# Second batch's rows 8 to 15 of the first stage in the prologue, fewer warm-up products, and loads on other queues

## The chip, the cores and the metric

The kernel runs on one core of one Trainium2 chip. The metric is the device time of the whole program in microseconds (us). Five engines work side by side, each with its own in-order instruction stream: TensorE (PE in the profile, with PEld for its weight loads), VectorE (DVE), ScalarE (ACT), GpSimd (POOL) and SyncE (SP). ACT, POOL and SP also issue DMAs; an issue on one of them stands in that engine's stream, and what is behind it waits with it.

## The reference

The input `x` has 8 batches of 3008 rows of 256 float32. Along the 3008 rows it is Fourier transformed, multiplied by a complex filter and transformed back; then an expert layer with 2048 hidden units runs over all 24064 rows.

```python
X = np.fft.rfft(x, axis=1)                    # (8, 1505, 256)
Y = X * (filt_r + 1j * filt_i)[None]
y = np.fft.irfft(Y, n=3008, axis=1).astype(np.float32).reshape(24064, 256)
h = y @ w_in                                  # (24064, 2048); the weights come in 64-bit floats
g = h - np.tanh(h)
out = (g @ w_out).astype(np.float32)          # (24064, 256)
```

## The kernel before

The length 3008 is 64 times 47. The transform of a batch has four steps: a 64-point step over every residue `r` (**first**), an exchange through DRAM (`ct1[b]`), a 47-point step there and back with the filter between (**middle**), another exchange (`ct2[b]`), and a last 64-point step (**last**, products `pu`, PSUM to SBUF tile `ut`). Residues `r` and 47-r are treated together, so there are 24 rows of them (`NH`), worked in groups of four (`NX` = 6 groups for the first step). The expert layer then takes `ut` in 48 groups of up to 512 rows, each in four units: `up` makes the hidden units (tile `h`), `shrink` applies h - tanh h with ACT and DVE, `down` multiplies by the second weights. From the second group on `up` uses seven products in place of eight (sums of weight blocks, `sums`, made on DVE); the first group (units 0 to 3) uses `up_plain` and `down_plain`.

The 64-bit weights are converted to float32 by hand: `converted` loads a piece (`raw`, `raws`, or halves of the tiles `ft` and `a2`), ACT makes its exponent (L181, tile `top` or `xy`), and DVE does six steps (L183 to L201). There are 16 pieces: `jobs[0]` to `jobs[4]` in the prologue (`early`, stepped by `convert`), `jobs[5]` on between the instructions of units 0 to 5 (`late`).

The **prologue** (pool `pro`, PSUM pool `ps0` with eight banks) does batch 0 by a way of its own. A few products on a constant (`warmer`, L1081) run first. Three chunks of eight rows of `x` (`xs[0..2]`) and of the matrix `f_d` (`fh`, copied to `f0` by DVE, L1188) are loaded over SP, ACT and POOL; `first0(c)` multiplies chunk c on PE (L1071), ACT copies it. The load of the filter on POOL waits for the first half of the third chunk (`gate`, L1197). Then come seven groups of frequencies: transposes (`across`, L1094), the 47-point step (`forth`, L428), the filter (`filtered`, DVE and POOL, L447 to L456), and the way back (`back0`, L1139 and L1141, and for the last group `back`, L478). ACT copies each of its results to a tile `e1` (four buffers, L1144 and L481), and a DMA stores that in `ct2[0]`. `rest` (L1129) loads `ct2[0]` back as the tile `e2` of the first `last`: frequencies 0 to 24 early, the last seven when the last stores have landed. In between, `first1` (L1227) does rows 0 to 7 of batch 1 with `f0`, ACT copies them, and SP stores them in `ct1[1]`. Eight more products of `warmer` follow, then `last` of the first group, then four products named `pt` (L1374), then unit 0 (L719).

The other rows of batch 1, and all of batch 2, are done by `first` (L308) between the units: ten jobs, taken from a list of due places (`due`). Everything is recorded in program order (a manual schedule), and the engines keep that order; the framework adds the semaphores. A pool that takes over the PSUM of a closed pool first waits for the closed pool's last readers: here `pu` waits for the last ACT copy of the prologue.

Of the kernel before, what the change touches and what calls it, by code (L numbers as in the profile page):

```python
# [21 lines left out]
SG = 5  # L22
# [95 lines left out]
def kernel(  # L118
# [144 lines left out]
    def load_x(t, b, r, n):  # L263

        nc.sync.dma_start(t[0:64, 0:n, :], dram(x.tensor, (b * SEQ + r) * DM,
                                                [[NR * DM, 64], [1, n * DM]]))
        lo = 1 if r == 0 else 0
        if lo:
            nc.sync.dma_start(t[64:128, 0, :], dram(x.tensor, b * SEQ * DM,
                                                    [[NR * DM, 64], [1, DM]]))  # L270
        nc.sync.dma_start(t[64:128, lo:n, :], dram(x.tensor, (b * SEQ + NR - r - lo) * DM,
                                                   [[NR * DM, 64], [-DM, n - lo], [1, DM]]))
        return t
# [310 lines left out]
    def last(i, z, held=False):  # L584
# [13 lines left out]
        even, odd = banks  # L598
        for k in (1, 0) if held else (1,):
# [3 lines left out]
        u4 = ut.rearrange("p h (j n) -> p h j n", n=128)  # L603
        m = sum(w == 128 for w in widths(c))
# [3 lines left out]
        if i == 0:  # L608
            uts[i] = (ut, None, w)
            yield  # L610
            return
# [420 lines left out]
    with tc.tile_pool(name="tr", bufs=2) as tr, tc.manual_schedule():  # L1032
# [16 lines left out]
        with tc.tile_pool(name="pro", bufs=1) as pro, \  # L1049
# [122 lines left out]
            for c in range(3):  # L1172
# [4 lines left out]
                (ACT if c else nc.sync).dma_start(fh, f_d[:, 512 * c:512 * c + 512])  # L1177
# [44 lines left out]
            def first1(x1):  # L1222

                for r in range(0, 8, 2):
                    pf = z0("pf", [128, 2, DM])
                    for k in range(2):
                        nc.tensor.matmul(pf[:, k], f0[:, r + k], x1[:, r + k],  # L1227
                                         start=True, stop=True)
                    if r % 4 == 0:
                        two = (tr.tile([128, 2, 2, DM], F32, tag="a1", bufs=1, name="a1") if r else  # L1230
                               buffer("xy").rearrange("p (m n) c -> p m n c", m=2))
                    a1 = two[:, r // 2 % 2]
                    ACT.copy(a1, pf)
                    nc.sync.dma_start(
# [288 lines left out]
```

## Time and profile before

| | us |
|---|---|
| median of 3 runs (lowest to highest) | 2541.87 (2540.63 to 2543.5) |
| the profiled execution | 2542.18 |
| its span, first to last instruction | 2540.3 |

| engine | busy us | share of the span |
|---|---|---|
| PE | 2522.6 | 99% |
| PEld (weight loads, beside PE) | 2173.1 | 86% |
| DVE | 1935.6 | 76% |
| ACT | 1694.2 | 67% |
| POOL | 1532.0 | 60% |

A row of the timeline gives the start, the length, the engine, the line, what it writes and reads, how many instructions are merged, and in brackets the idle time before it with what ended it. A float32 product shows as two matmul instructions (a product of 128x256 as two of 128x256). The prologue ends and the first unit of the expert layer begins at about 80 us.

### The profile page before, as it was taken

Reading aid. Unit: us, or ns where it says so; the run is one execution under the profiler, and the core shown is the slowest. Engines: PE = TensorE matmul, PEld = TensorE weight load, DVE = VectorE, ACT = ScalarE, POOL = GpSimd, SP = SyncE. Lnnn points to the kernel's source line nnn. Section 1 sums busy time; section 2 is a strip of 40 time slices with the busy share of each in tenths; the row PEclk is TensorE's granted clock in tenths of the full one; section 3 lists DMA queues with packets and bytes.
Section 4 is the critical chain, followed back from the end, with each engine's and each line's share of the span. In section 5 each row is a group of like instructions: output and inputs, shape, how many; then the busy total and the mean of one; then the engine's idle time right before and its main releaser. Section 6 shows DMA issues by size and latency. Waiting matters only on the chain.

```text
span 2540.3 us, 44575 instructions
## 1 busy us (share of the span) xinstructions
PE 2522.6 (99%) x17072; PEld 2173.1 (86%) x17072; DVE 1935.6 (76%) x2270; ACT 1694.2 (67%) x2551; POOL 1532.0 (60%) x1112
## 2 busy tenths in 40 slices
PE   9999999999999999999999999999999999999998
PEld 8678889888898888988888888898889888898887
DVE  6888877988678876888669886698866888555555
ACT  4666666667666766676667666666666666666665
POOL 5255665667556765676656665666655666455552
PEclk9999999999999999999999999999999999999999
DMA  9854224422343323342334322343123322110110
GB/s 245 261 150 117 65 54 100 112 65 53 86 108 91 82 69 89 80 112 59 80 87 105 87 56 72 96 111 89 36 72 84 92 66 53 26 31 19 25 22 19
DMA packets 333664, 211.37 MB, mean 83 GB/s; under 512 B 231645, under 2 KB 305531, under 8 KB 329793
## 3 DMA queue, kind: packets, MB, share of 16 engines
q1 hardware_dynamic: 319091, 184.93, 29.8%
q0 software_dynamic: 11120, 16.16, 2.3%
q10 hardware_dynamic: 3230, 7.34, 0.9%
q8 instruction: 136, 2.23, 0.4%
q14 instruction: 87, 0.71, 0.1%
HBM read 127.81 MB, written 83.39 MB: 83 GB/s over the span
## 4 chain that ended last, share of the span: by engine, by line
PE 96%; DVE 2%; DMA 1%; issue 0%; POOL 0%; ACT 0%; ACTq 0%; SPq 0%; POOLq 0%; DVEq 0%
PE o L821 44%; PE x L648 25%; PE z L648 12%; PE y L648 6%; PE pm L415 2%; PE pu L595 2%; PE pm L351 1%; PE o L883 1%; PE pf L308 1%; DMA filt<-in_filt_r_dram 1%; DMA x<-in_x_dram 0%; DMA ct<-e 0%; PE o L719 0%; PE x L719 0%; PE z L719 0%
## 5 line engine op out<-in xcount | busy, mean ns | idle before, releaser
L821 PE MATMUL o<-t,wd 128*128 128x256 f32 (+1 forms) x3008 | 762.7, 376 | 0.0
L619 POOL TENSOR_TENSOR t<-h 128x512 f32<-128x512 f32 (+1 forms) x184 | 303.6, 1650 | 707.3 <-DVE h L771 642.2
L771 DVE TENSOR_TENSOR h<-h,y 128x1024 f32<-128x1024 f32 (+1 forms) x384 | 571.0, 1487 | 156.4 <-ACT y L767 156.4
L821 PEld LDWEIGHTS o<-t,wd 128*128 128x128 f32 x3008 | 568.8, 190 | 84.5 <-POOL o L853 15.1
L648 PE MATMUL x<-tu,wu 128*128 128x256 f32 (+1 forms) x2256 | 571.4, 376 | 0.0
L821 PE MATMUL o<-h,wd 128*128 128x256 f32 (+1 forms) x2256 | 569.9, 375 | 0.2 <-DVE h L771 0.2
L648 PEld LDWEIGHTS x<-tu,wu 128*128 128x128 f32 x2256 | 427.4, 190 | 53.8 <-issue 3.9
L821 PEld LDWEIGHTS o<-h,wd 128*128 128x128 f32 x2256 | 428.3, 190 | 50.9 <-issue 0.8
L654 ACT COPY s<-x 128x512 f32<-128x512 f32 (+1 forms) x188 | 109.3, 581 | 517.4 <-PE x L648 517.3
L764 ACT ACTIVATE y<-y 128x1024 f32<-128x1024 f32 (+1 forms) x384 | 399.5, 1040 | 12.1
L767 ACT ACTIVATE y<-y 128x1024 f32<-128x1024 f32 (+1 forms) x384 | 399.8, 1041 | 4.6
L761 ACT ACTIVATE y<-h 128x1024 f32<-128x1024 f32 (+1 forms) x384 | 400.6, 1043 | 2.5 <-DVE h L697 1.7
L622 POOL TENSOR_TENSOR t<-h,t 128x512 f32<-128x512 f32 (+1 forms) x184 | 338.3, 1838 | 0.0
L620 POOL TENSOR_TENSOR t<-h,t 128x512 f32<-128x512 f32 (+1 forms) x184 | 310.5, 1688 | 14.4
L621 POOL TENSOR_TENSOR t<-h 128x512 f32<-128x512 f32 (+1 forms) x184 | 276.9, 1505 | 0.0
L654 ACT COPY u<-x 128x512 f32<-128x512 f32 (+1 forms) x376 | 214.1, 569 | 72.9 <-PE x L648 69.6
L697 DVE COPY h<-x 128x512 f32<-128x512 f32 (+1 forms) x188 | 127.6, 679 | 129.1 <-PE x L648 128.9
L689 DVE TENSOR_TENSOR h<-z,u 128x512 f32<-128x512 f32 (+1 forms) x188 | 127.2, 677 | 88.9 <-ACT u L654 88.5
L648 PE MATMUL x<-ut,wu 128*128 128x256 f32 (+1 forms) x752 | 194.0, 380 | 0.2 <-DVE h L697 0.2
L648 PE MATMUL z<-tu,wu 128*128 128x256 f32 (+1 forms) x752 | 190.2, 375 | 1.4 <-DVE h L705 1.4
L648 PE MATMUL y<-ut,wu 128*128 128x256 f32 (+1 forms) x752 | 190.1, 375 | 0.0
L648 PE MATMUL z<-ut,wu 128*128 128x256 f32 (+1 forms) x752 | 190.0, 375 | 0.0
(215 smaller groups left out, 2933.5 us busy)
## 6 DMA issues: line engine op xcount, KB each, us to landing
ft<-filt SPq DMA_DIRECT2D x28, 1024.0 KB
ct<-nn SPq DMA_DIRECT2D x56, 512.0 KB
e<-ct SPq DMA_DIRECT2D x47, 512.0 KB
a<-ct SPq DMA_DIRECT2D x112, 192.0 KB
out_dram<-ot SPq DMA_DIRECT2D x1248, 16.0 KB
x_sb<-in_x_dram SPq DMA_DIRECT2D x110, 128.0 KB
ct<-a SPq DMA_DIRECT2D x60, 128.0 KB
ct<-x_sb SPq DMA_DIRECT2D x60, 128.0 KB
```

The costliest lines, as they stand in the source:

```text
L619: by.tensor_sub(t[0], b[0][1], b[0][0])
L620: by.tensor_sub(t[1], b[1][1], t[0])
L621: by.tensor_sub(t[2], b[1][1], b[0][1])
L622: by.tensor_sub(t[3], b[1][0], t[1])
L648: nc.tensor.matmul(bank[:, k], wu[:, q - 1, (2 * u + k) * 128:(2 * u + k + 1) * 128], rhs[q - 1], start=(first and k == 0), stop=True, ski ...
L654: ACT.copy(t, X)
L697: V.tensor_copy(h[:, 2, :, 0:w], X)
L761: ACT.activation(y[k], ht[k], AF.Arctan, scale=TURN)
L764: ACT.activation(y[k], y[k], AF.Tanh, scale=BEND)
L767: ACT.activation(y[k], y[k], AF.Square, scale=SCALE, accum_out=y_sums[:, 2 * U + k // 2:2 * U + k // 2 + 1])
L771: V.tensor_mul(ht[k], ht[k], y[k])
L821: nc.tensor.matmul(product(q), wd[:, q - 1, (2 * u + k) * 128: (2 * u + k + 1) * 128], rhs[q - 1][:, k], start=(u == 0 and k == 0 and q == ...
```

## The change

- The first `warmer` has 7 products in place of 15; two more (on `f0`) stand between `first0(0)` and `first0(1)`. The `warmer` at the end of the prologue has 2 in place of 8, and 2 products `pt` stand in place of 4.
- The second piece of the matrix `f_d` is loaded by SP in place of ACT, between the first and the second chunk of `x`. The raw weights of `jobs[1]` (ACT before) and `jobs[2]` (POOL before) are loaded by SP, behind those of `jobs[0]`.
- Rows 8 to 15 of batch 1 are done in the prologue too: `x1b` (1 MB) is loaded by POOL at group 1, multiplied behind rows 0 to 7, copied by ACT into two blocks of `wu` that are not filled yet, and stored by POOL. Rows 0 to 7 are stored by POOL as well, in two DMAs in place of SP's four. `first` has two jobs fewer (eight), and `due` is spread over eight.
- The early `rest` is issued by POOL in place of SP, the late one by SP and ACT in turn in place of SP alone; it now stands behind rows 0 to 7 and ahead of rows 8 to 15.
- `last` of the first group copies and combines its result in two halves in place of one.

```diff
     def load_x(t, b, r, n, queue=nc.sync):
...
+        if i == 0:
+            t = tr.tile([128, 2, CH, 64], F32, tag="e1", bufs=2, name="odd")
+            for h in range(2):
+                ACT.copy(t[:, h], odd[:, h])
+                V.tensor_add(u4[:, h, :, 0:64], even[:, h], t[:, h])
+                V.tensor_sub(u4[:, h, 0:m, 127:63:-1], even[:, h, 0:m], t[:, h, 0:m])
+            uts[i] = (ut, None, n // 2)
+            yield
+            return
...
-                (ACT if c else nc.sync).dma_start(fh, f_d[:, 512 * c:512 * c + 512])
+                (ACT if c == 2 else nc.sync).dma_start(fh, f_d[:, 512 * c:512 * c + 512])
...
-            warmer(15, filt[2][:, 0])
+            warmer(7, filt[2][:, 0])
             first0(0)
+            warmer(2)
             first0(1)
-            began.append(begun(tiles0, jobs[0], queue=nc.sync))
-            began.append(begun(tiles0, jobs[1], queue=ACT))
-            began.append(begun(tiles0, jobs[2], queue=G))
+            began += [begun(tiles0, job, queue=nc.sync) for job in jobs[:3]]
...
-            def first1(x1):
-                for r in range(0, 8, 2):
+            def first1(x1, at, tiles):
+                for r in range(at, at + 8, 2):
                     pf = z0("pf", [128, 2, DM])
...
+                    if r % 4 == 0:
+                        two = tiles.pop(0)()
+                    ACT.copy(two[:, r // 2 % 2], pf)
+                    if r % 4:
+                        G.dma_start(dram(ct1[1], (r - 2) * DM, [[NH * DM, 128], [1, 4 * DM]]),
+                                    two.rearrange("p m n c -> p (m n c)"))
...
                 if g == 2:
-                    x1 = load_x(big([128, 8, DM], F32, "x1"), 1, 0, 8)
+                    load_x(x1, 1, 0, 8)
+                if g == 1:
+                    x1 = big([128, 8, DM], F32, "x1")
+                    x1b = load_x(big([128, 8, DM], F32, "x1b"), 1, 8, 8, G)
...
-            rest(0, SG * (last_g - 1), [nc.sync])
+            rest(0, SG * (last_g - 1), [G])
             way_back()
-            rest(SG * (last_g - 1), NA - SG * (last_g - 1), [nc.sync])
-            fs = first(2, z2, [(1, c) for c in range(2, NX)])
-            next(fs)
             convert(100)
-            for _ in first1(x1):
-                pass
+            first1(x1, 0, [lambda: buffer("xy").rearrange("p (m n) c -> p m n c", m=2),
+                           lambda: tr.tile([128, 2, 2, DM], F32, tag="a1", bufs=1, name="a1")])
+            rest(SG * (last_g - 1), NA - SG * (last_g - 1), [nc.sync, ACT])
+            fs = first(2, z2, [(1, c) for c in range(4, NX)])
+            next(fs)
+            first1(x1b, 8, [(lambda q=q: wu[:, q].rearrange("p (m n c) -> p m n c", m=2, n=2))
+                               for q in (4, 5)])
...
-            warmer(8)
+            warmer(2)
...
-            for _ in range(4):
+            for _ in range(2):
                 nc.tensor.matmul(warm[0:KM], mats[:, 3 * KM:4 * KM], mats[:, 3 * KM:3 * KM + 256],
...
-            due = [4 + (LEAD - 4) * k / (NX + 4) for k in range(NX + 4)]
+            due = [4 + (LEAD - 4) * k / (NX + 2) for k in range(NX + 2)]
```

The streams of two engines change where the prediction looks. PE at the start of the program, before; `warm` are the warm-up products, `x_87`, `x_97` and `x_106` the three chunks of `x`, `f` the matrix:

```order
L1081 MATMUL warm<-filt_79 128x256 x15
L1071 MATMUL pf<-f_80,x_87 128x128 x16
L1071 MATMUL pf<-f_80,x_97 128x128 x16
L1071 MATMUL pf<-f_80,x_106 128x128 x16
L1094 MATMUL pq<-one_sb,wd 120x128 x8
```

And now:

```order
L1086 MATMUL warm<-filt_79 128x256 x7
L1076 MATMUL pf<-f_80,x_87 128x128 x16
L1086 MATMUL warm<-f_80 128x256 x2
L1076 MATMUL pf<-f_80,x_97 128x128 x16
L1076 MATMUL pf<-f_80,x_106 128x128 x16
L1099 MATMUL pq<-one_sb,wd 120x128 x8
```

The first chunk's products stand behind 7 products in place of 15.

ACT at the end of the prologue, before; `ct` is `ct2[0]`, `e` the tiles `e1` (named `e_608` and `e_615` before, `e_606` and `e_613` now), and `odd` is half of the first `last`:

```order
L481 COPY e_608<-pe 112x2x128
L483 DMA ct_0<-e_608 48x2x128
L481 COPY e_615<-pe 112x2x128
L483 DMA ct_0<-e_615 48x2x128
L181 ACTIVATE top<-raws 128x512
L1233 COPY xy<-pf 128x512 x2
L1233 COPY a_665<-pf 128x512 x2
L601 COPY odd<-pu 128x512
```

And now (`e_450` is the tile `e2` of the first `last`):

```order
L481 COPY e_606<-pe 112x2x128
L483 DMA ct_0<-e_606 48x2x128
L481 COPY e_613<-pe 112x2x128
L483 DMA ct_0<-e_613 48x2x128
L181 ACTIVATE top<-raws 128x512
L1235 COPY xy<-pf 128x512 x2
L1235 COPY a_650<-pf 128x512 x2
L1134 DMA e_450<-ct_0 7x1024 x2
L1235 COPY wu<-pf 128x512 x4
L604 COPY odd<-pu 128x256 x2
```

Two loads of the late `rest` and the four copies of rows 8 to 15 now stand between the copies of rows 0 to 7 and `odd`.

More of the change, by code (lines that the diff above doesn't have):

```diff
@@ L598, in last @@
         even, odd = banks
+        u4 = ut.rearrange("p h (j n) -> p h j n", n=128)
+        m = sum(w == 128 for w in widths(c))
+        if i == 0:
[7 more added lines that the diff above has]
+            return
         for k in (1, 0) if held else (1,):
@@ L1220 @@
             first0(2)
[L1222 to L1224 removed]
+            def first1(x1, at, tiles):
+                for r in range(at, at + 8, 2):
                     pf = z0("pf", [128, 2, DM])
                     for k in range(2):
[L1227 removed]
+                        nc.tensor.matmul(pf[:, k], f0[:, r + k], x1[:, r + k - at],
                                          start=True, stop=True)
                     if r % 4 == 0:
[L1230 to L1234, printed above, removed]
[L1235 to L1236 removed]
+                        two = tiles.pop(0)()
[3 more added lines that the diff above has]
+                                    two.rearrange("p m n c -> p (m n c)"))
             a2 = {0: across(0)}
```

24 lines of the change are left out of this document (8 added, 16 removed).

## The prediction

> **What bounds the kernel now.** I read the page first, then the chain of waits, then the waits and timelines of the single engines in the first 200 us. The page's busy times and its shares of the chain:
>
> ```profile
> PE 2522.6 (99%) x17072; PEld 2173.1 (86%) x17072; DVE 1935.6 (76%) x2270; ACT 1694.2 (67%) x2551; POOL 1532.0 (60%) x1112
> ```
>
> TensorE is nearly never idle, so one would count removed products and be done. The prologue is different: the chain of waits there (start, length, what) passes through DMAs.
>
> ```profile
> 58.74 7.30 DMA ct<-e
> ...
> 66.12 0.59 ACT e L1144
> ...
> 68.43 0.38 ACT e L481
> ...
> 68.83 0.33 ACTq L483
> ...
> 69.65 3.61 DMA ct<-e
> ...
> 73.68 2.23 DMA e<-ct
> ...
> 76.05 0.33 PE pu L595 x4
> ...
> 76.71 1.15 PE pu L595 x60
> 77.86 1.92 PE pt L1374 x8
> ```
>
> The last stores of batch 0 land, are loaded back as `e2`, and only then can `pu` start. The reader is to see that TensorE has finished the prologue's products before that; what it does there costs nothing.
>
> Behind the prologue TensorE is busy without a gap, but the chain leaves it once more, at the first group with sums. Two pieces of the chain, and the busy times of that stretch (PE, PEld, DVE, ACT, POOL):
>
> ```profile
> 118.73 1.52 PE o L719 x4
> ...
> 121.66 0.49 ACT odd L601
> 122.14 0.02 issue
> 122.17 0.69 DVE ut L605
> ```
>
> ```profile
> 141.14 0.61 DVE h L697
> 141.75 0.04 issue
> 141.79 1.13 PE x L648 x4
> ```
>
> ```profile
> 79.60:141.80 62.20, 62.03 (x262) 38.03 (x261) 57.83 (x114) 42.59 (x70) 21.54 (x28) 1.00 0.92 277
> ```
>
> From 122.17 to 141.79 the chain is VectorE's: it converts weights and sums them, 57.83 us of work in 62.20, and at 141.79 TensorE waits for its copy of `h` (L697). Before the change both arrive there at nearly the same moment. So a product taken off TensorE ahead of 141.79 is worth only as much as VectorE also gets earlier.
>
> **The change part by part.** The profiled execution took 2542.18, 0.31 above the median of 2541.87; gains are worked out in the former's rows and taken off the median.
>
> *Start.* The products on the first chunks, the warm-up products in two windows (starts in brackets), the row of POOL's loads of `x` with their time to landing, and DVE's copies of the three pieces of the matrix:
>
> ```profile
> 10.72 10.88 PE L1071 MATMUL pf<-f,x 128*128 128x128 f32 x96
> ```
>
> ```profile
> 1.40:6.90 5.50, 5.45 (x13) 1.00 0.92 222
> 6.90:10.80 3.90, 3.90 (x19) 1.00 1.06 301
> ```
>
> ```profile
> 1.29 3.29 POOL L1184 DMA_DIRECT2D x<-in_x_dram  x5 [0.83 <-POOLq L1507]
> ```
>
> ```profile
> DMA to landing us min/median/max: 7.5/10.6/14.0
> ```
>
> ```profile
> 4.20 0.62 DVE L1188 COPY f<-fh 128x512 f32<-128x512 f32 x1 [2.42 <-DMA fh<-f]
> 11.10 0.43 DVE L1188 COPY f<-fh 128x512 f32<-128x512 f32 x1 [5.54 <-DMA fh<-f]
> 15.12 0.43 DVE L1188 COPY f<-fh 128x512 f32<-128x512 f32 x1 [3.20 <-DMA fh<-f]
> ```
>
> Warm-up now takes 14 instructions; the first window shows 13 in 5.5 us, so it ends near 7.1 in place of 10.72. One instruction of the first stage costs 10.88 / 96 = 0.113, a chunk 3.63. TensorE alone would end at 7.1 + 3.63 + 0.8 (four warm-up instructions at 3.90 / 19) + 7.26 = 18.8, in place of 21.60: 2.8 earlier. Data allow less: the last of POOL's five loads is issued at about 3.9 and, if it is the one that took 14.0, lands at 17.9; half a chunk (1.8) follows: 19.7, 1.9 earlier. The landings themselves move, since the second matrix piece leaves ACT's queue, where it and the third landed as late as 11.10 and 15.12, for a place behind SP's first chunk. I take 2.3, between both. The Trainium skill, page "DMA: Bandwidth & Descriptors", section "Issuing engines are not separate DMA queues", says that loads of all issuers share the same 16 engines and that another issuer saves only the time to issue. By that rule the landings stay and this term is 1.9, the time 2537.2; the 4.20 beside 11.10 above shows that the place in the queue counts, but no run here has it moved.
>
> Nothing downstream asks for more. A window of the prologue (PE, PEld, DVE, ACT, POOL):
>
> ```profile
> 40.00:60.00 20.00, 19.33 (x100) 16.39 (x101) 19.06 (x25) 8.90 (x17) 13.79 (x17) 1.00 0.86 244
> ```
>
> PE (19.33 of 20) and DVE (19.06) are both nearly without gaps, so the start of their chain moves its end. The three raw weights on SP stand behind all of `x` in that queue, and the filter on POOL now has one raw load fewer ahead of its second group.
>
> *1 MB more in the prologue.* `x1b` (POOL, at group 1) is the cost of this. The DMA summary of the first 90 us, and two windows (last two columns DMA share and GB/s):
>
> ```profile
> DMA packets 12464, 21.77 MB, mean 242 GB/s; under 512 B 1890, under 2 KB 7788, under 8 KB 12392
> ```
>
> ```profile
> 38.00:40.00 2.00, 1.50 (x7) 0.93 (x6) 1.97 (x4) 0.08 (x1) 0.68 (x1) 1.00 0.54 136
> 40.00:42.00 2.00, 1.36 (x6) 1.20 (x7) 1.93 (x4) 0.59 (x1) 1.71 (x3) 1.00 0.15 36
> ```
>
> At 242 GB/s it takes 4.3 us. The engines are free for some 2.6 us in these two windows, into which the load falls, and for less around 30. I take nothing for it; uncovered it costs up to 4.3. Issuing it costs POOL two instructions of 0.6 to 1.3 (five cost 3.29 above), ahead of its next one, which is due only at 39.33:
>
> ```profile
> 39.33 1.27 POOL nn L456
> ```
>
> *End of the prologue.* SP's store that lands last is issued at 69.65, though its tile was copied at 68.81: four loads of the early `rest` stand ahead of it on SP. They now stand on POOL, where the tail is free, so the store goes at 68.83 with ACT's half and lands 3.61 later, at 72.4. ACT then issues two loads (0.33 each, SP the other two) to 73.1, and behind them stand four copies of rows 8 to 15, for which `pu` waits (it takes over their PSUM). Their price is that of rows 0 to 7:
>
> ```profile
> 69.80 1.06 ACT L1233 COPY xy<-pf 128x512 f32<-128x512 f32 x2
> ```
>
> So copies end at 73.1 + 2.1 = 75.2, and `e2` lands at about 72.8 + 2.5 = 75.3. `pu` starts at 75.4, without the pause of 0.34, takes 1.3 and ends at 76.7 in place of 77.86: 1.1. TensorE's products of rows 8 to 15 (3.46, the price of rows 0 to 7) take the place of 12 warm-up instructions (2.6) ahead of that and are hidden; POOL's stores are needed only by `middle` of batch 1.
>
> *Behind the prologue.* Two jobs of `first` fewer, each of this price, and 0.96 of `pt`:
>
> ```profile
> 86.05 1.73 PE pf L308 x8
> ```
>
> TensorE could be 2 x 1.73 + 0.96 = 4.4 earlier at L697's place. VectorE has the same instructions in the same order; only its waits can shrink. All that the profile shows up to there, but one that VectorE causes itself, and what ScalarE was doing:
>
> ```profile
> 83.67 0.43 DVE L183 TENSOR_SCALAR xy<-xy 128x512 f32<-128x512 f32 x1 [0.52 <-ACT xy L181]
> 97.15 0.43 DVE L183 TENSOR_SCALAR xy<-xy 128x512 f32<-128x512 f32 x1 [0.61 <-ACT xy L181]
> 106.03 1.09 DVE L771 TENSOR_TENSOR h<-h,y 128x896 f32<-128x896 f32 x1 [0.37 <-ACT y L767]
> 122.17 0.69 DVE L605 TENSOR_TENSOR ut<-pu,odd 128x512 f32<-128x512 f32 x1 [0.22 <-ACT odd L601]
> ```
>
> ```profile
> 82.96 0.67 ACT L181 ACTIVATE xy<-ft 128x512 f32<-128x512 f32 x1 [3.86 <-DMA ct<-xy]
> 101.08 1.07 ACT L310 COPY a<-pf 128x512 f32<-128x512 f32 x2 [2.06 <-DMA ct<-a]
> ```
>
> The first goes because the store of `xy`, for which ACT waits 3.86, leaves earlier, on POOL; the next two because a job of `first` and its copies move behind them on ACT; the last with TensorE's lead. Together 1.7; the rest of the 4.4 becomes a wait of 2.7 on TensorE. The halves of the first `last` bring TensorE up to 0.7, of which VectorE sees nothing.
>
> Sum: 2.3 + 1.1 + 1.7 = 5.1. 2541.87 - 5.1 = 2536.8. With the start at 1.9 to 2.8, the end at 0.8 to 1.4 and the waits at 0.6 to 2.4 this case lies from 2535.3 to 2538.6.
>
> **The rivals.** A measurement of this kernel tells about 0.2%, 5.1 us, from no change: faster means below 2536.8, slower above 2547.
>
> 1. *VectorE does not hold TensorE.* Then all of the 4.4 counts: 2.3 + 1.1 + 4.4 = 7.8, 2534.1. For it: VectorE has 4.4 us of idle time in the 62.20. Against it: the chain is VectorE's for 20 us without a pause.
> 2. *The start does not pay.* DMAs are the limit from 2 to 29 us anyway, and the megabyte uses up what is gained: the 2.3 goes, 2.8 stay, 2539.1. For it: the store of 7.30 above shows how full the queues are at 58. Against it: the free windows.
> 3. *Slower: the megabyte stays ahead of the stores.* POOL's queue holds `x1b` ahead of the stores of `e1`, whose four buffers make ACT wait (the copy at 66.12 comes right behind such a landing). If the 4.3 us are not used up by 58, the copy at 66.12 is 4.3 late, the start's gain is gone with it, and the last store takes 7.30 as the one at 58.74 did in place of 3.61: 3.7 more, ahead of ACT's two loads, its four copies and so `pu`. 4.3 + 3.7 - 2.8 = 5.2 slower, 2547.1. It decides from 2.8 us of added landing on. Against it: shares of 0.54 and 0.15 at 38 to 42. The Trainium skill, page "TensorE: Matmul & The Clock Gate", section "Part 1: The HAM clock gate", adds that an idle window of about 3.4 us halves TensorE's clock for as long again; with 12 warm-up instructions fewer ahead of `pu` that would be 1.7 more, an estimate by that page; no run here shows it.
>
> **How the numbers follow.** My forecast has 0.48, about the likeliest sum's edge: 0.28 faster, 0.20 within 0.2%. Rival 1 has 0.20 (faster), rival 2 0.20 (within), rival 3 0.12 (slower). Faster 0.48, same 0.40, slower 0.12. The range runs from just under rival 1 to 2541.2, which holds rival 2 with 2 us of the megabyte on top, and leaves rival 3 out. The forecast alone: 2535.3 to 2538.6.
>
> **What would show it.** In the profile after, L1076's products end at 18.8 to 19.7 (21.60 means rival 2's start); `pu` ends near 74.4 by the profile's clock, 2.3 + 1.1 earlier; TensorE's waits between there and 140 name DVE `h` L702 (L697 before) with about 2.7 us in place of 0.2; if they do not and the time is below 2535, rival 1 holds. I am wrong at the root if `pu` starts later than 76.05, or if ACT's copies of `e` wait longer for `ct<-e` than before.

## The result, and the profile after

The changed kernel takes 2548.38 us (median of 20 runs, 2543.84 to 2552.58) where the kernel before, run beside it, takes 2542.85 (20 runs, 2540.63 to 2546.57). The ratio is 1.0021 with a 95% interval from 1.0015 to 1.0027: slower by about 5.5 us. The forecast was 2536.8, its range ended at 2541.2.

The profiled execution took 2548.66, its span is 2546.8. The page's busy times first:

```profile
PE 2520.6 (99%) x17044; PEld 2168.9 (85%) x17044; DVE 1933.9 (76%) x2272; ACT 1694.5 (67%) x2552; POOL 1537.2 (60%) x1121
```

TensorE does 2.0 us less than before (2522.6) and the span is 6.5 longer, so TensorE stands idle 8.5 us more. PE's timeline of the first 24 us shows the first of these waits (start, length, what, in brackets the idle time ahead and what ended it):

```profile
10.51 2.02 PE L1076 MATMUL pf<-f,x 128*128 128x128 f32 x16 [1.10 <-DMA x<-in_x_dram]
...
15.80 2.02 PE L1076 MATMUL pf<-f,x 128*128 128x128 f32 x16 [2.41 <-DMA x<-in_x_dram]
18.17 5.59 PE L1076 MATMUL pf<-f,x 128*128 128x128 f32 x48 [0.35 <-DMA x<-in_x_dram]
```

The warm-up is shorter, but TensorE then stands still for `x`, 3.86 us in three pieces. The products of the first stage end at 23.76 in place of 21.60. VectorE's copy of the second matrix piece, now loaded by SP:

```profile
13.86 0.43 DVE L1193 COPY f<-fh 128x512 f32<-128x512 f32 x1 [9.04 <-DMA fh<-f]
```

The second piece came at 11.10 before. In the middle of the prologue VectorE, which before waited only for the last group's filter (`filt_end`, 1.51 us), has four waits for the filters of the other groups (its timeline, the filter's lines):

```profile
57.95 1.23 DVE L447 TENSOR_TENSOR nn<-xy,filt 120x1024 f32<-120x1024 f32 x1 [4.24 <-DMA filt<-in_filt_r_dram]
59.57 0.69 DVE L452 TENSOR_TENSOR xy<-xy,filt 120x512 f32<-120x512 f32 x1 [0.39 <-DMA filt<-in_filt_i_dram]
63.96 1.23 DVE L447 TENSOR_TENSOR nn<-xy,filt 120x1024 f32<-120x1024 f32 x1 [2.37 <-DMA filt<-in_filt_r_dram]
66.02 0.69 DVE L452 TENSOR_TENSOR xy<-xy,filt 120x512 f32<-120x512 f32 x1 [0.83 <-DMA filt<-in_filt_i_dram]
69.59 0.69 DVE L447 TENSOR_TENSOR nn<-xy,filt_end 112x512 f32<-112x512 f32 x1
```

They are 7.83 us in all. Where they come from stands in SP's timeline, after and (second fence) before; `x` at L265 is the load of rows 0 to 7:

```profile
35.03 2.39 SPq L1127 DMA_DIRECT2D filt<-in_filt_i_dram  x3
37.52 7.71 SPq L1127 DMA_DIRECT2D filt_end<-in_filt_r_dram  x3
...
47.16 0.54 SPq L265 DMA_DIRECT2D x<-in_x_dram  x1
```

```profile
32.86 2.74 SPq L1122 DMA_DIRECT2D filt<-in_filt_i_dram  x3
35.70 3.04 SPq L1122 DMA_DIRECT2D filt_end<-in_filt_r_dram  x3
...
41.00 0.54 SPq L265 DMA_DIRECT2D x<-in_x_dram  x1
```

Three small loads (23 to 24 KB each) on SP stretch from 3.04 to 7.71 us, since SP waits between them for landings of its earlier loads (6.4 us in the longest wait), and every later load of SP, the filters of the last groups among them, is 6.2 us late (47.16 against 41.00). Of these, 2.2 were there already at the loads ahead of the three (35.03 against 32.86), from the late start. POOL issued the megabyte at 32.6 and 33.2.

The end of the prologue and the first unit, PE's timeline, a piece of the chain of waits, and ACT's last copy of `e`:

```profile
83.14 0.33 PE L595 MATMUL pu<-gt,e 64*64 64x64 f32 x4 [1.67 <-DMA e<-ct]
84.21 1.15 PE L595 MATMUL pu<-gt,e 64*64 64x64 f32 x60 [0.74 <-DMA e<-ct]
86.59 1.77 PE L724 MATMUL x<-ut,wu 128*128 128x448 f32 x4 [0.18 <-DVE ut L606]
...
145.34 1.13 PE L653 MATMUL z<-ut,wu 128*128 128x256 f32 x4 [1.21 <-DVE h L694]
147.06 1.91 PE L653 MATMUL x<-ut,wu 128*128 128x256 f32 x4 [0.59 <-DVE h L702]
...
196.69 1.13 PE L653 MATMUL z<-tu,wu 128*128 128x256 f32 x4 [1.09 <-DVE h L710]
```

```profile
73.30 0.38 ACT e L481
73.68 0.02 issue
73.70 4.66 DMA ct<-e
```

```profile
74.18 0.37 ACT L481 COPY e<-pe 112x256 f32<-112x256 f32 x1 [0.51 <-PE pf L1231]
```

Three lines of before that were not shown yet, to lay beside them (VectorE's and PE's timelines):

```profile
62.47 0.69 DVE L447 TENSOR_TENSOR nn<-xy,filt_end 112x512 f32<-112x512 f32 x1 [1.51 <-DMA filt_end<-filt]
```

```profile
79.77 1.77 PE L719 MATMUL x<-ut,wu 128*128 128x448 f32 x4
...
189.77 1.13 PE L648 MATMUL z<-tu,wu 128*128 128x256 f32 x4 [1.12 <-DVE h L705]
```

Place by place, after against before: the first stage ends 2.16 late; the last filter step starts 7.12 late (69.59 against 62.47); `pu` ends 7.50 late (85.36 against 77.86); unit 0 starts 6.82 late (86.59 against 79.77); the products at L653 that wait for `h` L702 start 5.27 late (147.06 against 141.79); the next place where TensorE waits for `h` in both 6.92 late (196.69 against 189.77); the span ends 6.5 late. So the start loses 2.2, the middle about 5, the end of the prologue 0.4, the shorter `pt` and the halves together give back 0.7, TensorE's lead behind the prologue gives back 1.55, and something between 147 and 197 takes 1.65 away again. That last step stands in the windows of this stretch (PE busy, PEld, DVE, ACT, POOL, then TensorE's granted clock, as a share of full speed):

```profile
144.00:145.00 1.00, 0.13 (x1) 0.00 (x0) 1.00 (x4) 0.00 (x0) 0.00 (x0) 1.00 0.78 142
145.00:146.00 1.00, 0.66 (x3) 0.61 (x4) 0.97 (x4) 0.00 (x0) 0.00 (x0) 1.00 0.77 157
146.00:147.00 1.00, 0.47 (x3) 0.07 (x1) 1.00 (x4) 0.00 (x0) 0.00 (x0) 1.00 0.89 181
147.00:148.00 1.00, 0.94 (x3) 0.76 (x4) 1.00 (x3) 0.00 (x0) 0.00 (x0) 0.63 1.07 234
148.00:149.00 1.00, 1.00 (x4) 0.82 (x3) 0.61 (x2) 0.00 (x0) 0.00 (x0) 0.50 1.03 250
149.00:150.00 1.00, 1.00 (x3) 0.79 (x3) 0.00 (x0) 0.99 (x2) 0.00 (x0) 0.50 1.05 240
150.00:151.00 1.00, 1.00 (x4) 0.67 (x3) 0.21 (x1) 0.97 (x2) 0.00 (x0) 0.66 1.06 274
```

TensorE is busy for 1.26 of the three us from 144 to 147, and then its clock is halved: 0.37 + 0.50 + 0.50 + 0.34 = 1.71 us of full clock are lost, which is the 1.65. The chain of waits says the same: behind the wait it is TensorE's alone for more than 40 us in both profiles, and its first three pieces take 1.91, 1.71 and 1.56 us where before they took 1.13, 0.86 and 1.50.

### The profile page after: what moved, and what is told of

Its sections match the earlier page's. It is cut to its first block, busy times and chain, and to the rows that moved or that the text cites. A ratio compares the mean times of both kernels' runs of the same rounds, so it can differ in the third digit from the quotient of the medians.

```text
span 2546.8 us, 44520 instructions
## 1 busy us (share of the span) xinstructions
PE 2520.6 (99%) x17044; PEld 2168.9 (85%) x17044; DVE 1933.9 (76%) x2272; ACT 1694.5 (67%) x2552; POOL 1537.2 (60%) x1121
## 4 chain that ended last, share of the span: by engine, by line
PE 94%; DMA 3%; DVE 2%; issue 0%; POOL 0%; ACT 0%; SPq 0%; ACTq 0%; POOLq 0%; DVEq 0%
PE o L826 44%; PE x L653 25%; PE z L653 12%; PE y L653 6%; PE pm L415 2%; PE pu L595 2%; DMA filt<-in_filt_i_dram 1%; DMA filt<-in_filt_r_dram 1%; PE pm L351 1%; DMA x<-in_x_dram 0%; DVE h L776 0%; PE pf L308 0%; PE o L888 0%; DMA a<-in_moe_w_out_dram 0%; DMA ct<-e 0%
## 5 line engine op out<-in xcount | busy, mean ns | idle before, releaser
L653 PE MATMUL x<-tu,wu 128*128 128x256 f32 (+1 forms) x2256 | 571.3, 376 | 0.0
L653 PEld LDWEIGHTS x<-tu,wu 128*128 128x128 f32 x2256 | 427.4, 190 | 54.1 <-issue 4.2
L625 POOL TENSOR_TENSOR t<-h,t 128x512 f32<-128x512 f32 (+1 forms) x184 | 311.0, 1690 | 14.4
L659 ACT COPY u<-x 128x512 f32<-128x512 f32 (+1 forms) x376 | 214.1, 569 | 73.5 <-PE x L653 70.2
L702 DVE COPY h<-x 128x512 f32<-128x512 f32 (+1 forms) x188 | 127.6, 679 | 129.3 <-PE x L653 129.1
L653 PE MATMUL x<-ut,wu 128*128 128x256 f32 (+1 forms) x752 | 194.7, 382 | 0.6 <-DVE h L702 0.6
L653 PE MATMUL z<-tu,wu 128*128 128x256 f32 (+1 forms) x752 | 190.2, 375 | 1.4 <-DVE h L710 1.4
L653 PE MATMUL z<-ut,wu 128*128 128x256 f32 (+1 forms) x752 | 190.1, 375 | 1.2 <-DVE h L694 1.2
L653 PE MATMUL y<-ut,wu 128*128 128x256 f32 (+1 forms) x752 | 191.0, 377 | 0.0
```

The costliest lines, as they stand in the source:

```text
L625: by.tensor_sub(t[1], b[1][1], t[0])
L653: nc.tensor.matmul(bank[:, k], wu[:, q - 1, (2 * u + k) * 128:(2 * u + k + 1) * 128], rhs[q - 1], start=(first and k == 0), stop=True, ski ...
L659: ACT.copy(t, X)
L702: V.tensor_copy(h[:, 2, :, 0:w], X)
```

## The experiments

Two theories stood after the result. **M**: the megabyte of rows 8 to 15 makes SP's filter loads late. **Q**: SP's queue is late by itself, since the matrix piece and three raw loads were put on it. The start, the end of the prologue and the clock were taken apart beside them. Every experiment ran beside the kernel before, whose median was 2542.67 beside no_mb, mb_g2, fh1_act and start_before; 2542.86 beside no_mb_stores, no_mb_rest, tail_warm and start_only; 2543.14 beside mb_only, after_warm, best and best_start; 2542.50 beside mb_last and best_start2. The ratios and intervals are to these. Each run has one profile, and places in two profiles of one kernel differ too: in best_start and best_start2 `pu` ends at 76.24 and 76.99.

**Without rows 8 to 15 in the prologue (no_mb).**

```diff
-                    x1b = load_x(big([128, 8, DM], F32, "x1b"), 1, 8, 8, G)
...
-            first1(x1b, 8, [(lambda q=q: wu[:, q]...) for q in (4, 5)])
...
-            fs = first(2, z2, [(1, c) for c in range(4, NX)])
+            fs = first(2, z2, [(1, c) for c in range(2, NX)])
...
-            due = [4 + (LEAD - 4) * k / (NX + 2) for k in range(NX + 2)]
+            due = [4 + (LEAD - 4) * k / (NX + 4) for k in range(NX + 4)]
```

> The changed kernel without rows 8 to 15 in the prologue (no 1 MB load, no products or copies of them; the first step of batch 1 has ten jobs between the units again). Theory M (the megabyte, issued at 32.6, stands beside SP's filter loads of the fourth group, issued from 32.55, which then land late; SP issues its next loads only when these have landed, and VectorE waits for the filters of the last groups): VectorE's waits for filters at L447 and L452, 7.8 us now, fall below 2, and the products pu end near 80 in place of 85.4. The two jobs cost 3.5 again on TensorE, of which the 1.6 us of waits on h and the stretch of lower clock at 147 to 150.6 (1.7) give back nearly all: 2543.5 (2542.5 to 2545). Rival Q (SP's queue itself is late, since the matrix piece and three raw loads were put on it): the waits for filters stay above 6, pu ends at 85, the time is 2548 or more.

It took 2545.82 us (ratio 1.0010, 1.0001 to 1.0020), 0.8 over M's range. In its profile no filter but the last group's is waited for, and that for 0.19: the group that waited 4.24 starts L447 at 53.19 without a pause, SP's load of rows 0 to 7 goes at 40.88, and the last filter step starts at 62.73. M holds for the middle, Q is out: the raw loads and the matrix piece are still on SP. The first stage ended late here too (23.19), so without the megabyte the middle takes up nearly all of such a start; the kernel before waits 1.51 for the last filter there anyway. But `pu` is late all the same, for another reason (PE's timeline, then the windows with the granted clock as third number from the end):

```profile
79.13 0.48 PE L595 MATMUL pu<-gt,e 64*64 64x64 f32 x4 [6.49 <-DMA f<-f_both]
80.33 1.97 PE L595 MATMUL pu<-gt,e 64*64 64x64 f32 x60 [0.72 <-DMA e<-ct]
```

```profile
74.00:76.00 2.00, 0.00 (x0) 0.00 (x0) 1.90 (x4) 0.00 (x0) 0.00 (x0) 1.00 0.98 303
...
84.00:86.00 2.00, 2.00 (x4) 1.01 (x3) 1.90 (x5) 0.15 (x1) 0.00 (x0) 0.50 0.89 301
```

The first row names `f_both`, which `pu` does not read; the second names the load of `e2`. The filter step is 0.26 late, the end of `pu` (82.30) 4.4: with the megabyte away, the change's other parts lose 4.2 us between these two. The DMA engines are full from 74 on (0.98 from 74 to 76, where before had 0.28), and TensorE, idle since 72.6, falls to half clock at 76.1.

**The megabyte one group later (mb_g2).** `x1b` is loaded beside `x1` at group 2; nothing else.

> The changed kernel with the 1 MB load issued one group later on POOL, behind the stores of the second group, near 44 us in place of 32.6. Theory M: SP's filter loads of the fourth group land before it and SP's stream is not held, so the filter waits on VectorE fall from 7.8 to about 2 to 3 (the megabyte now shares with the loads of x1 and of the fifth group's filter), pu ends near 81, the time is 2543 to 2545. Rival Q: no change, 2548.

2545.18 us (1.0014, 1.0004 to 1.0023). The filter waits were 2.76, 1.42 and 2.41, 6.6 in all, and `pu` ended at 82.2. The time is a little over the range of M, and the filter waits did not fall to 2 or 3: the later place moved them. SP's load of rows 0 to 7 is in time (39.33), as M says. Its profile's first stage was done at 21.87, by chance, since its start is that of the changed kernel; how much of the 3.2 us on the median comes from the later place is not shown. A later load is no free load.

**The matrix piece on ACT again (fh1_act).**

```diff
-                (ACT if c == 2 else nc.sync).dma_start(fh, f_d[:, 512 * c:512 * c + 512])
+                (ACT if c else nc.sync).dma_start(fh, f_d[:, 512 * c:512 * c + 512])
```

> The changed kernel with the second piece of the matrix on ACT's queue again, ahead of the third; nothing else. Theory S (its place on SP behind the first chunk of x made it land at 13.86 in place of 11.10, and pushed the second chunk of x behind it): copied near 11.1, TensorE's waits at the second chunk (2.4 and 0.35 us) fall below 1, the products of the first stage end at 19.5 to 21 in place of 23.76; if the start carries to the end, 2545 to 2546. Rival (the landings of x alone count, the queues are full from 2 to 29 us anyway): they end at 23 or later, 2548.

One row of PE, one of VectorE:

```profile
12.90 7.54 PE L1076 MATMUL pf<-f,x 128*128 128x128 f32 x64
```

```profile
10.86 0.43 DVE L1193 COPY f<-fh 128x512 f32<-128x512 f32 x1 [6.26 <-DMA fh<-f]
```

The second and third chunk run through without a wait and end at 20.44, 3.3 earlier than in the changed kernel. The other profiles bear out the direction, with a smaller size: in the six kernels with the short warm-up and the piece on SP the stage ends at 21.87 to 24.08 (23.2 on average; the latest has a stretch at half clock in it), in the five with the short warm-up and the piece on ACT at 20.44 to 21.36 (21.0). Theory S holds: the piece's place on SP was the start's loss, about 2 us. At unit 0 3.2 of this profile's lead were left (83.36). The median is 2546.72 (ratio 1.0016, 1.0006 to 1.0026), 0.7 over S's range and 1.7 below the changed kernel's; the two intervals overlap, so a gain in time is not shown.

**The whole start as before (start_before).** 15 warm-up products, the matrix piece on ACT, the raw loads on SP, ACT and POOL.

> The changed kernel with the whole start as it was: 15 warm-up products and none between, the second matrix piece on ACT, the raw loads on SP, ACT and POOL. The first stage's products end at 21.6 in both theories. Theory M: the megabyte still delays the filters, the middle keeps its loss of 5, the time is 2546 (2545 to 2547). Rival Q: with the raw loads off SP the filter waits go as well, 2541 to 2543.

2548.13 us (1.0024, 1.0014 to 1.0035), no gain on the median. The profiled run was its fastest, 2544.36: first stage done at 21.35, a wait of 3.50 for the fifth group's filter all the same, and one of 3.68 at the next group, where a piece of the filter lands at 61.64 and VectorE starts at 61.76 (its row names an ACT copy that ends no earlier than VectorE's start). Q is out a second time. The time lies above the 2547 that M allowed; the other eight runs have a lower mean clock than the profiled one (0.998 or 0.997 against 0.999), and none of them has a trace.

**The stores of rows 0 to 7 back on SP (no_mb_stores), and the last loads of `e2` back on SP alone (no_mb_rest).** Both are no_mb with one more part undone.

```diff
+            held1 = []
...
-                        G.dma_start(dram(ct1[1], (r - 2) * DM, ...), two...)
+                        held1.append((dram(ct1[1], (r - 2) * DM, ...), two...))
...
             next(fs)
+            for d, s in held1:
+                nc.sync.dma_start(d, s)
```

```diff
-            rest(SG * (last_g - 1), NA - SG * (last_g - 1), [nc.sync, ACT])
+            rest(SG * (last_g - 1), NA - SG * (last_g - 1), [nc.sync])
```

> The changed kernel without rows 8 to 15 in the prologue, as in no_mb, and with the two stores of rows 0 to 7 (512 KB each) on SP behind the loads of x_sb, where they stood in the kernel before, in place of POOL. Theory E1 (in no_mb these stores go at 72.3 and 73.2, ahead of the last loads of e2 at 73.0 to 74.7, and fill the DMA engines: those loads take 5.8 in place of 2.2): the loads of e2 land within 2.5 to 3 of their issue, pu ends at 78 to 79 in place of 82.3, TensorE waits less than 4 us before it, and the time falls by 3 to 4 from no_mb's 2545.8 to 2542. Rival E2 (the loads are late because ACT issues half of them beside SP's loads of x_sb): they still take over 5, pu ends at 82, 2545.8.

> The changed kernel without rows 8 to 15 in the prologue, as in no_mb, with all four of the last loads of e2 on SP, ahead of x_sb, as in the kernel before; the stores of rows 0 to 7 stay on POOL. Theory E1 (the stores on POOL fill the DMA engines): the loads of e2 still take over 4.5, pu ends at 81 to 82, the time stays at 2545 to 2546. Rival E2 (ACT's two loads fall behind x_sb): the loads land within 3, pu ends at 78 to 79, 2542.

PE in no_mb_stores:

```profile
76.47 0.33 PE L595 MATMUL pu<-gt,e 64*64 64x64 f32 x4 [2.96 <-DMA e<-ct]
77.77 1.97 PE L595 MATMUL pu<-gt,e 64*64 64x64 f32 x60 [0.96 <-DMA e<-ct]
```

The last loads of `e2`, issued from 73.31 to 74.70, landed by 77.77: 3.1 behind the last issue, where no_mb took 5.6 (74.71 to 80.33). From the last filter step to the end of `pu` it took 16.3 us (63.44 to 79.74) in place of 19.6. So far E1 fits: POOL's two stores of 512 KB, issued at 72.26 and 73.23 in no_mb, stood ahead of the loads. no_mb_rest looks as short from its last filter step (65.59 to 81.58, 16.0), but that step was itself late there, 3.08 of it a wait for `filt_end`. A better start for the count is the end of ACT's last copy of `e`, whose store `e2` waits for. From it to the end of `pu` it takes 9.1 us in the kernel before (68.80 to 77.86), 10.8 in the changed kernel (74.55 to 85.36), 12.5 in no_mb (from 69.85), 11.0 in no_mb_rest (from 70.55) and 8.9 in no_mb_stores (from 70.84). Over all profiles, the seven kernels with the stores of rows 0 to 7 on POOL take 10.8 to 12.7 but for fh1_act (8.8); eight that leave them on SP take 7.5 to 9.1 but for tail_warm (10.2, at half clock); mb_last (10.6) has sixteen product instructions more there. So E1 holds in the traces: taking the stores off POOL gave 3.5 us in the one pair that differs in nothing else, no_mb and no_mb_stores. E2 has at most the 1.4 between no_mb and no_mb_rest. In time neither is shown: the medians, 2544.90 and 2545.30 (ratios 1.0006, 0.9997 to 1.0016, and 1.0006, 0.9996 to 1.0016), are too near to no_mb's to tell, and the 2542 that E1 forecast for no_mb_stores did not come.

**Fewer warm-up products at the end of the kernel before (tail_warm).** 2 in place of 8 ahead of `pu`, 2 `pt` in place of 4.

> The kernel before with 2 warm-up products in place of 8 at the end of the prologue and 2 products pt in place of 4; nothing else. Theory C (TensorE's idle stretch ahead of pu halves its clock, as in no_mb where it idled 6.5 us and ran at 0.50 from 77 to 86): the idle stretch grows from 2.4 to about 5, the granted clock falls to 0.5 for some us from 75 or 76 on, and the time is 2 to 3 longer, 2545. Rival (the idle stretch is harmless; the removed products only covered it): the clock stays 1.00, the time is 2542.5, or up to 1 less for the two products pt.

The windows of its profile, the granted clock as third number from the end:

```profile
74.00:76.00 2.00, 0.18 (x4) 0.21 (x4) 1.90 (x4) 0.00 (x0) 0.00 (x0) 0.78 0.35 86
76.00:78.00 2.00, 1.80 (x60) 1.64 (x61) 0.74 (x2) 0.00 (x0) 0.00 (x0) 0.50 0.94 293
...
80.00:82.00 2.00, 2.00 (x5) 0.84 (x4) 1.90 (x5) 0.00 (x0) 0.00 (x0) 0.52 1.07 312
```

Theory C holds for the mechanism and fails on its price. The clock is halved from 75.1 to 81.9, but the median is 2543.47, 0.6 over the kernel before (1.0001, 0.9992 to 1.0011), no difference. In the profile unit 0 starts 0.6 late (80.38), the products that wait for `h` in the kernel before 1.05 late (142.84 against 141.79) and the place at 189.77 0.9 late (190.71). So the price was about 1 us there in place of 2 to 3. One reason is in the kernel: two products `pt`, 0.96 us, are missing in that stretch; the rest is not taken apart.

**The short warm-up at the start alone (start_only).** The kernel before with 7 products and 2 behind the first chunk.

> The kernel before with 7 warm-up products in place of 15 and two more behind the first chunk; every load as before. Theory S (with the second matrix piece on ACT the start pays): the first stage's products end at 20.0 to 20.6 in place of 21.6, the prologue's end moves by the same 1.0 to 1.6, and the time is 2541 to 2541.7. Rival (VectorE's middle or the loads of the filter on POOL, which wait for the gate at 15.4, take it up): L447 starts earlier by 1 but pu does not, 2542.7.

The first stage ended at 21.16, 0.44 earlier, not the 1.0 to 1.6 expected: TensorE waited for `x` 0.36, 1.29 and 0.20. VectorE's timeline in the middle:

```profile
60.93 0.69 DVE L452 TENSOR_TENSOR xy<-xy,filt 120x512 f32<-120x512 f32 x1 [3.83 <-DMA ct<-e]
```

It waits now, there and 1.38 us at the group before (the row names `ct<-e`; the instruction reads the filter, whose last piece lands at 60.80), and `pu` ended at 78.51, 0.65 later than before. The rival holds in this profile: the middle takes it up. 2541.88 us (0.9997, 0.9988 to 1.0007) is no difference.

**The megabyte alone (mb_only).** The kernel before with this, rows loaded and not used:

```diff
-                    x1 = load_x(big([128, 8, DM], F32, "x1"), 1, 0, 8)
+                    load_x(x1, 1, 0, 8)
+                if g == 1:
+                    x1 = big([128, 8, DM], F32, "x1")
+                    x1b = load_x(big([128, 8, DM], F32, "x1b"), 1, 8, 8, G)
```

> The kernel before with the 1 MB load of rows 8 to 15 added on POOL at group 1, and nothing else: the rows are loaded and not used, all ten jobs stay. Theory M (the load alone makes SP's filter loads late): VectorE waits 5 to 8 us in all for filters at L447 and L452 where it waited none, pu ends at 81.5 to 83 in place of 77.86, the time is 2546 to 2547.5. Rival (it takes a late start or the raw loads on SP as well): waits below 2, pu ends below 79, the time is 2543.

2549.28 us, 6.1 over the kernel before (1.0021, 1.0012 to 1.0030): one added load costs as much as the whole change. (The parts do not add up: no_mb, the change without this load, is 3.2 over the kernel before, and both together are 5.5.) VectorE's waits, SP's timeline, and what SP waited for from 28 to 62 (total, times, longest):

```profile
57.68 1.23 DVE L447 TENSOR_TENSOR nn<-xy,filt 120x1024 f32<-120x1024 f32 x1 [5.22 <-DMA filt<-in_filt_r_dram]
61.95 0.69 DVE L452 TENSOR_TENSOR xy<-xy,filt 120x512 f32<-120x512 f32 x1 [3.04 <-DMA filt<-in_filt_i_dram]
```

```profile
36.14 5.71 SPq L1122 DMA_DIRECT2D filt_end<-in_filt_r_dram  x3
...
47.98 0.54 SPq L265 DMA_DIRECT2D x<-in_x_dram  x1
```

```profile
SPq L1122 <- DMA filt<-in_filt_r_dram: 5.6, 2, 4.5
SPq L1122 <- DMA filt<-in_filt_i_dram: 2.5, 1, 2.5
```

M is shown, with nothing of the start or of the raw loads in the kernel, and a size over its expectation: `pu` ends at 85.27, 7.4 late (in a run of 2550.76, the longest of the eleven). SP's filter loads of the fourth group were issued at 30.46, as before, but SP could go on only when they had landed, and they landed while the megabyte was on its way (its two loads take 12.4 and 14.4 us to land). The windows from 38 to 42 of before and of mb_only show why the load costs more than its bytes (DMA share and GB/s at the end):

```profile
38.00:42.00 4.00, 2.87 (x13) 2.13 (x13) 3.90 (x7) 0.66 (x2) 2.38 (x3) 1.00 0.35 86
```

```profile
38.00:42.00 4.00, 2.88 (x14) 2.14 (x13) 3.90 (x7) 0.74 (x2) 1.26 (x1) 1.00 1.05 172
```

The engines are full at 172 GB/s, not at the 242 of the mean by which I priced the load. And SP's next loads start 7 us late (47.98 against 41.00).

**The changed kernel with its tail warm-up restored (after_warm).** 8 and 4 products in place of 2 and 2.

> The changed kernel with 8 warm-up products in place of 2 at the end of the prologue and 4 products pt in place of 2. Theory C (part of the changed kernel's time is stretches at half clock that its shorter warm-ups let in): the mean granted clock of its runs rises toward 0.999 and the time falls by 1 or more from 2548.4, although TensorE has 3.5 us of products more. Rival (the stretches come from the waits in the middle of the prologue and on h, which no warm-up covers): clock as in the changed kernel, 2548 to 2549.5.

2548.62 us (1.0021, 1.0012 to 1.0030), mean clocks of 0.997 to 0.999 as in the changed kernel. Theory C falls for the changed kernel: with the warm-up back, its profile still has two half-clock stretches (a mean clock of 0.59 from 86 to 90 and 0.83 from 150 to 160), one behind TensorE's waits for `e2`, one behind its waits for `h`.

**The parts that gained (best, best_start, best_start2).** best is the kernel before with the early `rest` on POOL and the first `last` in halves; best_start adds the short warm-up of start_only; best_start2 is best_start again.

> The kernel before with two of the change's parts alone: the early rest issued by POOL, and the first last in two halves. All theories: SP's store of the last e1 goes at 68.9 in place of 69.65, pu ends 0.5 to 0.9 earlier; the halves bring unit 0 another 0.7 closer behind pu; VectorE's chain starts earlier by both. 2541.2 to 2542 where the kernel before has 2542.7. It would be no gain if VectorE then waits for weights loaded at the old time.

> As best, with the shorter warm-up of start_only (7 products and 2 behind the first chunk, the matrix piece on ACT). If the 0.4 to 1 us of the first stage carry through the middle, 0.5 to 1 below best: 2540.5 to 2541.2. In start_only they were lost to the filter of the fifth group, which VectorE waited for; then it equals best.

> best_start once more, beside mb_last and for the interval of its ratio to the kernel before, which reached from 0.9983 to 1.0001: if the gain of 1.4 to 1.9 us holds, 2541.4 and a ratio of 0.9992 again; if it was chance, 2542.7.

In best's profile `pu` ends at 76.90, 1.0 earlier, and unit 0 starts at 78.65, 1.1 earlier; TensorE then waits for `h` (0.22, 0.24 and 0.59 before 142) and the place at 189.77 stands at 189.96. The times were 2541.47 (0.9994, 0.9985 to 1.0003), 2541.36 (0.9992, 0.9983 to 1.0001) and, a second time, 2542.70 (1.0001, 0.9992 to 1.0010). No version was shown to beat the kernel before.

**The megabyte behind the filter loads from the inputs (mb_last).** best_start with rows 8 to 15 in the prologue, loaded by SP at group 4 (with the other edits named below):

```diff
+                if g == 4:
+                    x1b = load_x(big([128, 8, DM], F32, "x1b"), 1, 8, 8)
...
```

> best_start with rows 8 to 15 in the prologue all the same, but their 1 MB loaded by SP behind all the filter loads (about 54 us), the stores of rows 0 to 7 on SP behind x_sb, one warm-up product in place of 8 at the end (their sixteen product instructions stand there), and eight jobs behind. Theory M (the megabyte costs through the filters, and only ahead of them): no waits for filters beyond best_start's, pu within 2.5 of best_start's 76.2, TensorE waits 1.5 to 2.5 on h behind the prologue, the time is 2541 to 2543: what the two jobs give is lost on that wait. Rival (a megabyte costs 4 to 6 wherever it stands, since the DMA engines are full from 45 to 66 as well, and the stores of e1 then land late): pu ends at 80 or later, 2545 to 2547.

2549.32 us (1.0029, 1.0017 to 1.0041). `pu` ends at 87.32, as the rival said, but the price is over its range, and its path is only half of what the trace shows. SP's, VectorE's and ACT's timelines:

```profile
56.97 1.11 SPq L1109 DMA_DIRECT2D filt_end<-filt  x2
```

```profile
71.25 0.69 DVE L447 TENSOR_TENSOR nn<-xy,filt_end 112x512 f32<-112x512 f32 x1 [9.39 <-DMA ct<-e]
```

```profile
71.57 0.58 ACT L1149 COPY e<-pe 120x512 f32<-120x512 f32 x1 [9.19 <-DMA ct<-e]
```

The megabyte, issued at 55.6 and 56.2, stands on SP ahead of the stores of `e1`, and ACT stands still for 9.19 us until the first of these has landed (71.47). It also stands ahead of the last pieces of the last group's filter, which SP copies into `filt_end` at 57.0 and 57.7, so it was not behind all that the filters need. These pieces land at 70.83 and 71.03, and VectorE, whose next step reads them, waits 9.39 (its row names `ct<-e`). The filters of the other groups cost 1.60. So the load delayed whatever SP had issued behind it, stores and filter alike, and this run does not choose between the two theories. In this prologue the load had no free place at any of the three points tried (32.6, 44 and 55.6).

## Why the prediction was wrong, point by point

**The start: wrong in sign.** Forecast 2.3 earlier, measured 2.16 later. The step that failed is the one on the landings: I took them to lie where they did, and let the matrix piece's new place on SP count for nothing. fh1_act shows what it counts: 3.3 us in that pair of profiles, about 2 on average over all of them. Even then the stage ends at 20.44, behind the 19.7 that I called the latest, since the shorter warm-up meets `x` that has not landed. My rule that the start's gain reaches the chain's end was not borne out: in start_only 0.44 gained became 0.65 lost in the middle, and in no_mb a loss of 1.6 became one of 0.26, though in fh1_act 3.2 of 3.3 were left at unit 0. The prediction cited the Trainium skill, page "DMA: Bandwidth & Descriptors", section "Issuing engines are not separate DMA queues", by which another issuer saves only the time to issue. The runs agree with its first half, that all share the same engines (POOL's megabyte delays SP's loads), and not with the second for a queue that is already long: the same piece was there at 10.86 to 12.24 from ACT (ten profiles) and at 12.57 to 13.86 from SP (six), where fh1_act issued it at 1.51 and the changed kernel at 2.47, only 0.96 later.

**The megabyte: the step that decides.** The prediction took nothing for it, with 4.3 as the most it could cost (its bytes by the mean rate of 242 GB/s) and the engines' free time at 38 to 42 as cover. It costs about 6 alone (mb_only). Taken out of the changed kernel (no_mb) it gives back only 2.6, since the two jobs return and the end of the prologue then loses more. Both halves of that step failed. The rate in that place is 172 GB/s, so there is more to hide; and the bound by bytes is no bound, since SP's stream waits for landings, so that three 24 KB loads became a delay of 7 us for all behind them. The free windows that I counted as cover were SP's own pause: from 36 to 42 it waits twice, 3.1 us in all, for a filter load of its own to land, and has only loads of 23 to 24 KB to issue until 41.00. Filled, they make SP late.

**Rival 3** named the right culprit and the wrong victim. In the changed kernel no copy of `e` waits longer; the filters do. In mb_last, where the load stands later and on SP, a copy waits for a store as it said, with the last filter late beside it. Its price (5.2 slower) was near the measured 5.5 by another way, which is luck. The sign that I had named for being wrong at the root came true: `pu` starts at 83.14, later than 76.05.

**The end of the prologue: wrong.** Forecast 1.1 earlier. From ACT's last copy of `e` to the end of `pu` it took 10.8 us against 9.1 before, 1.75 later; from the last filter step it is only 0.4 (15.8 against 15.4), since TensorE's products for it wait 0.50 for VectorE now, where before they stood behind others. SP's store does go at once behind its copy, as forecast (73.68 and 73.70), but it lands in 4.66 and not 3.61, and `e2` lands late. The step that failed is the one on POOL's stores: I said they were needed only later, and did not ask what they fill. In the pair no_mb and no_mb_stores they cost 3.5 us there. best, which has the early `rest` on POOL without these stores, takes 8.3 from the last copy of `e` to the end of `pu`, 0.7 less than before; this half of the forecast was right in direction.

**Behind the prologue: right, and then taken back.** Forecast 1.7 for the lead of 4.4, the rest a wait on `h` of 2.7. Measured from the end of `pu` to 147.06: 2.2, of which 0.7 ahead of unit 0, with waits on `h` of 1.21 and 0.59. The 0.7 is not the halves' alone: best, with the halves and four products `pt`, has 1.75 between `pu` and unit 0, where before has 1.91 and the changed kernel 1.23. Rival 1 is out. What I did not see is that such a wait can cost more than itself: the half-clock stretch behind it took 1.65 back in the profiled run. It is not in each run: mb_g2, fh1_act and start_before have waits there of 0.94 to 1.42 and 0.60, and full clock from 140 to 160.

**The clock.** Sorted by mean clock, the changed kernel's runs take 2546.3 at 0.999 (4 runs), 2547.7 at 0.998 (11) and 2550.5 at 0.997 (5), the kernel before 2542.7 at 0.999 (15 runs) and 2543.7 at 0.998 (17), by means and with the runs beside mb_only. So some 4 of the 5.5 us remain at equal clock (3.6 and 4.0), and the rest goes with the lower clock; which waits lower it in runs without a trace stays open. The Trainium skill, page "TensorE: Matmul & The Clock Gate", section "Part 1: The HAM clock gate", has a free-running window of about 3.4 us; here TensorE's clock fell 3.4 to 5 us behind its last product (tail_warm 71.7 to 75.1, mb_last 65.2 to 70.2), which agrees. The stretch at 147 came without so long an idle time. The estimate by that page beside rival 3, a stretch at half clock ahead of `pu`, did not come in the changed kernel's profile: TensorE idled 1.67 there and kept its clock.

## What to carry to other kernels

A load that nothing waits for is priced by what stands behind it on the shared DMA engines, and by the in-order issuer that waits for those landings, not by its bytes over a mean rate: here 1 MB on its own cost 6 us in a stage whose DMA engines showed idle windows. An idle window of the DMA engines is cover only if their next user is not the one that made it; follow that queue's next ten issues first. And when one engine's work is cut while another holds it, the gain turns into idle time, which may cost clock on top.

## What the runs showed of the hardware that was not expected

- Half-clock stretches ahead of the program's end came in three lengths, 3.41, 6.83 and 10.24 us, which is one, two and three times the first (after: 147.3 to 150.7; tail_warm: 75.1 to 81.9; no_mb: 76.1 to 86.4; mb_last: 70.2 to 80.4).
- A stretch needs no long idle time ahead: 1.26 us of products in 3 us were not enough to keep the clock (after, 144 to 147, longest wait 1.21), while the same two waits kept it in mb_g2 and fh1_act.
- A long stretch at half clock can cost little: 6.8 us of it made tail_warm's profile 0.9 us late at 190, and no difference in the median is shown.
- The DMA engines were full at 172 GB/s in one stretch (mb_only, 38 to 42) and at 388 GB/s in another (before, 62 to 64: share 1.04).
